# Transposing probabilities in two halves by rows, with the causal masks behind them

## The chip, the cores and the metric

The kernel runs on one core of a Trainium2 chip. Its time is device microseconds of one execution. The engines are named as the profile names them: PE (TensorE; its weight loads are PEld), DVE (VectorE), ACT (ScalarE), POOL (GpSimd) and SP (which here issues the DMAs). L612 is line 612 of the kernel.

## The reference, cut to what matters

Decayed causal attention over 8 x 8 heads of 576 tokens and 64 columns, in float32, and a feed-forward layer behind it:

```python
scores = (1.0 / np.sqrt(D)) * np.matmul(q, k.transpose(0, 1, 3, 2))
cum = np.cumsum(np.log(np.clip(f, 0.0001, 1.0)), axis=-1)
decay = cum[:, :, :, None] - cum[:, :, None, :]
scores = np.where(causal, -1000000000.0, scores + decay)   # causal: column > row
attn = np.exp(scores - np.max(scores, axis=-1, keepdims=True))
attn = attn / (np.sum(attn, axis=-1, keepdims=True) + 1e-09)
x = np.matmul(attn, v)                                     # then (4608, 512)
h = x @ w_in
y = (h * erf(softplus(h))) @ w_out
```

## The kernel before, in words

The program has two stages. The first is attention, 64 steps t = 0 to 63 and a few that drain the pipeline. The second is the feed-forward layer, of which a unit has 36 matmuls into y (L242) and up to 42 into four banks (L184). The y matmuls take as weights the gate tiles (gh and gl, L225 to L232), which lie on the right side of SBUF behind the four small tiles `line0` to `line3` (L341).

A step of attention works on one half of a pair of heads: p, half = t // 2, t % 2. The 576 query rows of a head are cut into five blocks; an even step has the blocks 4 and 1, an odd step 3, 2 and 0. Both heads of the pair, j = 0 and 1, are done side by side. For a given half the work goes through six steps:

- `scores(t)`, L528: the two heads' products with q and k on 64 rows of the array each, into two buffers s0 and s1 of two PSUM banks; there are just these two buffers, so step t + 1 writes over what step t left. Right behind them (L544) matmuls of 128 rows with a constant add the mask of the diagonal blocks: two in an even step from t = 2 on, four in an odd one.
- `reduce(t, j)`, L561: DVE adds the decay, writes the sum to `pr` and finds the row's bound; two (even) or three (odd) instructions a head.
- `exps(t, j)`, in step t + 1: the exponentials on ACT.
- `normalize(t)`, in step t + 2: a sum and a reciprocal on DVE, then four or six products on POOL.
- `transposes(t, a)`, in step t + 3: the probabilities are transposed on PE, 128 x 128 each, into bank a: 12 of them for an even t (a = 0, 1, 2), 13 for an odd one, whose short bank 3 comes first. Three PSUM buffers (tag "t") take turns. `evacuate(t, a)` copies the banks to `pt`: ACT does 0, 1 and 3 and bank 2 of an even t, DVE bank 2 of an odd one.
- `values(t)`, in step t + 4: matmuls with 64 columns of the array for each head (L630); `store` copies the result on DVE.

So even steps transpose an odd half, with bank 3, and odd steps an even half. Steps 0 to 2 also have `lead(4)`, four filler matmuls behind the masks, and step 0 has `spread` (four matmuls that ACT copies to the decays). On the side DVE, ACT and POOL convert the weights (`words`, `joined`, `out_high` and others).

Every engine's order is the order in which the code issues (a manual schedule). PE goes through scores, masks, transposes, values; DVE through normalize, store, reduce (j = 0), reduce (j = 1), bank 2, conversions; ACT through exps (j = 0), the first evacuations, exps (j = 1), the other evacuations. The array has three modes: 64 rows (scores), 128 rows (masks, transposes) and 64 columns (values).

Of the kernel before, what the change touches and what calls it, by code (L numbers as in the profile page):

```python
# [11 lines left out]
F32 = mybir.dt.float32  # L12
# [10 lines left out]
P = 128  # L23
# [8 lines left out]
END = [64, 192, 320, 448, 576]  # L32
PAD = 64

BLOCKS = [[4, 1], [3, 2, 0]]


TOFF = {4: 0, 1: 1152, 3: 0, 2: 896, 0: 1536}
TCOLS = [1536, 1664]
# [3 lines left out]
SCOL = {4: 192, 1: 0, 0: 448, 3: 0, 2: 512}  # L43


BANKS = [[[(4, 0, 0), (4, 0, 1), (4, 0, 2), (4, 0, 3)], [(4, 1, 0), (4, 1, 1), (4, 1, 2), (4, 1, 3)],
# [274 lines left out]
def attention_moe(ctx, tc, q2, k2, vp, f, w_in, w_out, out):  # L321
    nc = tc.nc
# [7 lines left out]
    ident = const.tile([P, P], F32, name="ident")  # L330
    make_identity(nc, ident)
    eye = const.tile([P, P], BF16, name="eye")
# [5 lines left out]
    upper = const.tile([P, P], BF16, name="upper")  # L338
    nc.vector.tensor_copy(out=upper, in_=low)
    edge = ctx.enter_context(tc.tile_pool(name="edge", bufs=1, side="right"))  # L340
    lines = [edge.tile([P, 32 if n else 24], F32, name=f"line{n}") for n in range(4)]  # L341
    for line in lines:
        nc.vector.memset(line, 1e-9)
    cum_d = dram.tile([B * H, S], F32, name="cum_d")
# [19 lines left out]
    def queue_transfers():  # L364
        for out, in_ in moves:
            nc.sync.dma_start(out=out, in_=in_)
        moves.clear()
# [102 lines left out]
    with ExitStack() as ph:  # L470
        early = ExitStack()
        wk = ph.enter_context(tc.tile_pool(name="wk", bufs=2))
        io = early.enter_context(tc.tile_pool(name="io", bufs=3, side="right"))
        ps_s = early.enter_context(tc.tile_pool(name="ps_s", bufs=2, space=PSUM, side="right"))
        ps_t = ph.enter_context(tc.tile_pool(name="ps_t", bufs=3, space=PSUM))
# [11 lines left out]
        pairs, stats, probs, vals, raw_scores, pts, banks, held = {}, {}, {}, {}, {}, {}, {}, {}  # L487
# [40 lines left out]
        def scores(t):  # L528


            p, half = divmod(t, 2)
            q, k = pairs[p][:2]
            s = [ps_s.tile([P, 1024], F32, name=f"s{t}_{j}", tag="s") for j in range(2)]
            for at, i, k0, k1 in PARTS[half]:
                for j in range(2):
                    h = slice(64 * j, 64 * j + 64)
                    nc.tensor.matmul(out=s[j][:, at:at + k1 - k0], lhsT=q[h, PAD + START[i]:PAD + END[i]],  # L537
                                     rhs=k[h, k0:k1], start=i > 0, stop=k1 < END[i] or i == 4 and p > 0)
            for j in range(2):
                for i in BLOCKS[half]:  # L540
                    if i == 3 or i == 4 and p:
                        continue
                    first = max(0, START[i])
                    nc.tensor.matmul(out=s[j][:, SCOL[i] + first:SCOL[i] + END[i]], lhsT=eye,  # L544
                                     rhs=upper[:, first - START[i]:], start=False, stop=True)
            raw_scores[t] = s
            probs[t] = wk.tile([P, TCOLS[half]], F32, name=f"pr{t}", tag=f"pr{half}")
            n = len(BLOCKS[half])
            stats[t] = lines[t % 4][:, :6 * n].rearrange("p (a j m) -> p a j m", a=3, j=2)

        def mask(p, i):

# [4 lines left out]
        def row(t, i, j):  # L557

            return probs[t][:, TOFF[i] + j * END[i]:TOFF[i] + (j + 1) * END[i]]

        def reduce(t, j):  # L561
            p, half = divmod(t, 2)
            c, s, st = pairs[p][2], raw_scores[t][j], stats[t]
            for m, i in enumerate(BLOCKS[half]):
                to, score, decay_ = (x.rearrange("p (k n) -> p k n", n=64) for x in (
                    row(t, i, j), s[:, SCOL[i]:SCOL[i] + END[i]], c[:, j, :END[i]]))
                nc.vector.tensor_tensor_reduce(  # L567
                    out=to[:, ::-1] if j else to, in0=score, in1=decay_, scale=-0.125, scalar=BIG,
                    op0=ALU.add, op1=ALU.min, accum_out=st[:, 0, j, m:m + 1])
            if j:  # L570
                del raw_scores[t]
                if half:
                    del pairs[p]

        def exps(t, j):
            st = stats[t]
            for m, i in enumerate(BLOCKS[t % 2]):
                seg = row(t, i, j)
                nc.scalar.activation(out=seg, in_=seg, func=AF.Exp, bias=st[:, 0, j, m:m + 1], scale=-1.0,  # L579
                                     accum_out=st[:, 1, j, m:m + 1])  # L580
# [13 lines left out]
        def transposes(t, a):  # L594

            half = t % 2
            if t not in pts:
                pts[t] = wk.tile([P, 1600 if half else 1536], F32, name=f"pt{t}", tag=f"pt{half}", bufs=1)
            banks[t, a] = b = ps_t.tile([P, 512], F32, name=f"t{t}_{a}", tag="t")
            for n, (i, j, *ch) in enumerate(BANKS[half][a]):  # L600

                at = TOFF[i] + (i * P if j is None else 2 * END[i] - ch[0] * P - P if j else ch[0] * P)
                nc.tensor.transpose(out=b[:, n * P:(n + 1) * P], in_=probs[t][:, at:at + P], identity=ident)  # L603

        def evacuate(t, a):
            b, pt = banks.pop((t, a)), pts[t]
            if a == 3:
                (nc.vector.tensor_copy if t == NH - 1 else nc.scalar.copy)(out=pt[:, 1536:], in_=b[:, 64:128])
            elif a == 2 and t % 2 or t == NH - 1:
                nc.vector.tensor_copy(out=pt[:, 512 * a:512 * a + 512], in_=b)  # L610
            else:
                nc.scalar.copy(out=pt[:, 512 * a:512 * a + 512], in_=b)  # L612
            if a == (3 if t == NH - 1 else 2):
                del probs[t]

# [46 lines left out]
        first = wk.tile([P, 2, P], F32, name="first", tag="pr1")[:B * H]  # L662
# [22 lines left out]
        for t in range(NH + 2):  # L685
            there = [0 <= t - n < NH for n in range(6)]
            p, half = divmod(t, 2)
            if half == 0 and there[2]:
                load_values(p - 1)
            if half == 0 and t + 4 < NH:  # L690
                load(p + 2)
                load_decays(p + 2)
            queue_transfers()
            if t == X0:
                moe.load_x(0)
                moe.later = moe.x_steps(0)
            if half and NH - 32 < t < NH - 16:
                moe.load_wi_part(*divmod((t - NH + 32) // 2, 4))
            if there[2]:
                normalize(t - 2)  # L700
            if half and t + 1 < NH:
                mask(p + 1, 4)
            if there[5] and t < NH + 2:
                store(t - 5)
            if t >= NH:
                units(t)
            if there[0]:
                scores(t)
            if t == 0:
                spread(pairs[0][2], cum)  # L710
            if t < 3:
                lead(4)
            if there[1]:
                exps(t - 1, 0)
            if there[0]:
                reduce(t, 0)
            if there[3]:
                order = range(3) if half else (3, 0, 1, 2)
                for a in order:
                    transposes(t - 3, a)  # L720
                for a in order[:-2]:
                    evacuate(t - 3, a)
            if there[4]:
                values(t - 4)
            if there[1]:
                exps(t - 1, 1)
            if there[0]:
                reduce(t, 1)
            if there[3]:
                for a in range(1, 3):  # L730
                    evacuate(t - 3, a)
            if there[0] and not half:
                mask(p, 3)
            todo = work.pop(t, [])
            while t > X0 and moe.later:
                step = moe.later[0]
                if (half if step[0] == moe.high else not half or columns(todo + [step]) > LIMIT):
                    break
                todo.append(moe.later.pop(0))
                if not half:  # L740
                    break
            convert(todo)
            if t > NH and there[4]:
                store(t - 4)
            if t == NH - 1:
                moe.load_x(1)
            if t == NH - 1:
                early.close()
                moe.ep = moe_pools.enter_context(tc.tile_pool(name="ep", bufs=2, side="right", reuse_waits="tile"))
                moe.ps_h = moe_pools.enter_context(tc.tile_pool(name="ps_h", bufs=1, space=PSUM, side="right", reuse_waits="tile"))  # L750
# [75 lines left out]
```

## Time and profile before

| | |
|---|---|
| median of 3 runs | 1083.06 us (1082.73 to 1083.41) |
| the profiled execution | 1082.37 us |
| its span, first to last instruction | 1080.5 us |
| granted PE clock | 1.00 |
| PE busy | 1073.0 us, 99% of the span |
| DVE, ACT, POOL busy | 829.2, 745.1 and 733.6 us |
| attention stage | to about 330 us |

A line of the timeline has the start, the length, the engine, the line of the code, the operation, out<-in, the shape and a count of equal instructions that follow each other; in brackets stand the idle time before it and what ended it. A float32 matmul of scores or values leaves two records, a transpose one. A matmul's end is modelled, and the next one can start before it. A line of a group ends in busy us, mean ns of one, and the engine's idle us before it.

### The profile page before, as it was taken

To read this page: it belongs to the slowest core of one execution; us is meant where nothing else is said; L and a number is where in the kernel's file an instruction comes from. 1 tells how busy PE (TensorE), PEld (TensorE's weight loads), DVE (VectorE), ACT (ScalarE), POOL (GpSimd) and SP (SyncE) were. 2 spreads that over 40 slices of the span, in tenths; PEclk is the share of its full clock that TensorE was granted. 3 is DMA by queue.
4 is the path that set the end of the run, shared out by engine and by line. 5 is a ranking of instruction groups with operands and counts; after the bars stand their busy time and mean duration, and the time that the engine had idled before them with its cause. 6 is when DMAs were issued, how large, how long until landed. Compare 5 with 4: busy or idle time off the path is not lost.

```text
span 1080.5 us, 21954 instructions
## 1 busy us (share of the span) xinstructions
PE 1073.0 (99%) x7480; PEld 944.3 (87%) x7480; DVE 829.2 (77%) x1878; ACT 745.1 (69%) x1624; POOL 733.6 (68%) x887
## 2 busy tenths in 40 slices
PE   8999999999999999999999999999999999999998
PEld 6888888888889899889889988988998899889887
DVE  6888888887667988987887986686766767676665
ACT  5898988998877657666665666566566655656553
POOL 3786998989856879698887878555363455536322
PEclk9999999999999999999999999999999999999999
DMA  8888999998747697878969787686858668684742
GB/s 290 280 297 278 352 315 331 349 315 299 257 144 266 234 333 265 327 291 286 341 245 340 259 299 273 229 319 221 308 182 304 261 233 303 237 317 165 250 181 98
DMA packets 87055, 293.69 MB, mean 272 GB/s; under 512 B 8992, under 2 KB 25376, under 8 KB 74912
## 3 DMA queue, kind: packets, MB, share of 16 engines
q1 hardware_dynamic: 86800, 292.00, 76.1%
q8 instruction: 60, 0.98, 0.3%
q14 instruction: 51, 0.42, 0.1%
q10 hardware_dynamic: 144, 0.29, 0.1%
HBM read 240.73 MB, written 51.53 MB: 270 GB/s over the span
## 4 chain that ended last, share of the span: by engine, by line
PE 95%; ACT 2%; DVE 2%; issue 1%; POOL 0%; POOLq 0%; ACTq 0%; DVEq 0%
PE y L242 37%; PE pha L184 9%; PE phy L184 9%; PE phx L184 9%; PE s L537 9%; PE o L630 8%; PE t L603 7%; PE phb L184 5%; PE s L544 1%; ACT pr L579 1%; DVE pr L567 1%; ACT pt L612 1%; PE lead L510 1%; ACT whi L425 0%; DVE wtop L393 0%
## 5 line engine op out<-in xcount | busy, mean ns | idle before, releaser
L231 POOL TENSOR_TENSOR gl<-e,gh 128x384 fp32r<-128x384 f32 x192 | 217.2, 1160 | 267.4 <-PE y L242 172.4
L242 PE MATMUL y<-wo,gh 128*128 128x512 f32 x1152 | 361.5, 395 | 0.1
L242 PEld LDWEIGHTS y<-wo,gh 128*128 128x128 f32 x1152 | 216.3, 189 | 47.4 <-DVE ys L263 0.8
L242 PE MATMUL y<-wo,gl 128*128 128x512 f32 x576 | 227.8, 396 | 0.0
L263 DVE TENSOR_TENSOR ys<-y,ys 128x512 f32<-128x512 f32 x252 | 171.7, 686 | 54.0 <-PE y L242 53.4
L591 POOL TENSOR_SCALAR pr<-pr,line 128x576 f32<-128x576 f32 (+4 forms) x320 | 170.7, 554 | 44.1 <-DVE line L587 23.8
L579 ACT ACTIVATE pr<-pr,line 128x576 f32<-128x576 f32 (+3 forms) x320 | 177.2, 562 | 2.2 <-DVE line L567 2.2
L567 DVE CUSTOM_DVE_ANT_0 pr<-s,c 128x576 f32<-128x576 f32 (+3 forms) x320 | 136.7, 487 | 50.7 <-issue 14.3
L230 ACT CAST gh<-e 128x384 fp32r<-128x384 f32 x192 | 94.1, 513 | 86.1 <-DVE e L223 79.2
L242 PEld LDWEIGHTS y<-wo,gl 128*128 128x128 f32 x576 | 108.5, 188 | 25.2
L213 ACT ACTIVATE e<-u 128x384 f32<-128x384 f32 x144 | 75.0, 522 | 76.6 <-DVE u L190 72.5
L184 PE MATMUL pha<-xs,wi 128*128 128x384 f32 x576 | 116.0, 336 | 0.0
L184 PE MATMUL phy<-xs,wi 128*128 128x384 f32 x576 | 115.4, 335 | 0.0
L184 PE MATMUL phx<-xs,wi 128*128 128x384 f32 x576 | 115.3, 335 | 0.0
L223 DVE TENSOR_TENSOR e<-e,u 128x384 f32<-128x384 f32 x144 | 114.3, 795 | 0.0
L537 PE MATMUL s<-k,q 64*128 64x320 f32 (+4 forms) x768 | 110.7, 407 | 1.5 <-DVE line L567 1.1
L612 ACT COPY pt<-t 128x512 f32<-128x512 f32 x158 | 88.5, 582 | 31.2 <-PE t L603 30.9
L184 PEld LDWEIGHTS pha<-xs,wi 128*128 128x128 f32 x576 | 102.0, 188 | 4.4
L630 PEld LDWEIGHTS o<-pt,v 128*64 128x64 f32 x1920 | 93.7, 137 | 11.4 <-DVE line L567 7.6
L630 PE MATMUL o<-pt,v 128*64 128x128 f32 (+1 forms) x1920 | 102.5, 259 | 0.5 <-DVE xo L639 0.5
L213 ACT ACTIVATE e<-pha 128x384 f32<-128x384 f32 x48 | 23.6, 491 | 114.3 <-PE pha L184 114.3
L184 PEld LDWEIGHTS phx<-xs,wi 128*128 128x128 f32 x576 | 101.2, 188 | 0.0
(75 smaller groups left out, 1733.0 us busy)
## 6 DMA issues: line engine op xcount, KB each, us to landing
wi<-wi_d SPq DMA_DIRECT2D x46, 1792.0 KB, 7.5
wo<-wo_d SPq DMA_DIRECT2D x48, 1024.0 KB, 5.4
v<-in_vp_dram SPq DMA_DIRECT2D x32, 576.0 KB, 4.6
r<-xt_d SPq DMA_DIRECT2D x48, 384.0 KB, 9.1
c<-cum_d SPq DMA_DIRECT2D x62, 288.0 KB, 6.7
q<-in_q_dram SPq DMA_DIRECT2D x32, 320.0 KB, 5.0
k<-in_k_dram SPq DMA_DIRECT2D x32, 288.0 KB, 6.2
part_d<-ys SPq DMA_DIRECT2D x36, 256.0 KB, 6.2
```

What stands on the lines that cost most here:

```text
L184: nc.tensor.matmul(out=ps, lhsT=wi[:, w, n, kd], rhs=xs[:, x, kd], start=not part and kd == 0 and i == 0, stop=kd == 1 and i == 2, skip_gr ...
L213: nc.scalar.activation(out=e_, in_=h[c], func=AF.Softplus)
L223: nc.vector.tensor_mul(e_, e_, h_)
L231: nc.gpsimd.tensor_tensor(out=gl, in0=e_, in1=gh.bitcast(F32), op=ALU.subtract)
L242: nc.tensor.matmul(out=y, lhsT=x[:, cs], rhs=wo[:, i, w], start=i == 0 and n == 0, stop=i == 1 and n == 2)
L263: nc.vector.tensor_tensor(out=ys, in0=y, in1=ys, op=ALU.add)
L537: nc.tensor.matmul(out=s[j][:, at:at + k1 - k0], lhsT=q[h, PAD + START[i]:PAD + END[i]], rhs=k[h, k0:k1], start=i > 0, stop=k1 < END[i] or ...
L567: nc.vector.tensor_tensor_reduce(out=to[:, ::-1] if j else to, in0=score, in1=decay_, scale=-0.125, scalar=BIG, op0=ALU.add, op1=ALU.min, ...
L579: nc.scalar.activation(out=seg, in_=seg, func=AF.Exp, bias=st[:, 0, j, m:m + 1], scale=-1.0, accum_out=st[:, 1, j, m:m + 1])
L591: nc.gpsimd.tensor_scalar(out=seg, in0=seg, scalar1=st[:, 2, j, m:m + 1], scalar2=1.0, op0=ALU.mult, op1=ALU.mult)
L612: nc.scalar.copy(out=pt[:, 512 * a:512 * a + 512], in_=b)
L630: nc.tensor.matmul(out=o[h, to:to + width], lhsT=v[:, ch, h], rhs=pt[:, at[j]:at[j] + width], start=n == 0, stop=n == len(parts) - 1, skip ...
```

## The change: what it does

Of the 12 or 13 transposes of a step the eight of banks 0 and 1 are each done as two halves: 64 rows of the probabilities with a 64 x 64 corner of the identity, so that a half gives 64 columns. The upper rows' halves go to bank 0 and the lower rows' to bank 1, in turn. They are in the 64-row mode of the scores and are issued right behind them. The masks, now a function of their own, follow the halves; then bank 3 (even steps) and bank 2 as before. In steps 0 to 2, which have no transposes, the masks follow `lead(4)`. The copies of the banks 0 and 1 put every run of 64 back in its place. `line3` is 64 instead of 32 columns wide, by which the tiles behind it on that side move by 128 bytes.

```diff
-    lines = [edge.tile([P, 32 if n else 24], F32, name=f"line{n}") for n in range(4)]
+    lines = [edge.tile([P, (24, 32, 32, 64)[n]], F32, name=f"line{n}") for n in range(4)]
...
+        def mask_scores(t):
+            p, half = divmod(t, 2)
             for j in range(2):
                 for i in BLOCKS[half]:
                     if i == 3 or i == 4 and p:
                         continue
                     first = max(0, START[i])
-                    nc.tensor.matmul(out=s[j][:, SCOL[i] + first:SCOL[i] + END[i]], lhsT=eye,
+                    nc.tensor.matmul(out=raw_scores[t][j][:, SCOL[i] + first:SCOL[i] + END[i]], lhsT=eye,
                                      rhs=upper[:, first - START[i]:], start=False, stop=True)
...
-            banks[t, a] = b = ps_t.tile([P, 512], F32, name=f"t{t}_{a}", tag="t")
-            for n, (i, j, *ch) in enumerate(BANKS[half][a]):
-
-                at = TOFF[i] + (i * P if j is None else 2 * END[i] - ch[0] * P - P if j else ch[0] * P)
-                nc.tensor.transpose(out=b[:, n * P:(n + 1) * P], in_=probs[t][:, at:at + P], identity=ident)
+            for n in (a, a + 1) if a == 0 else (a,) if a > 1 else ():
+                banks[t, n] = ps_t.tile([P, 512], F32, name=f"t{t}_{n}", tag="t")
+            pieces = [TOFF[i] + (i * P if j is None else 2 * END[i] - ch[0] * P - P if j else ch[0] * P)
+                      for n in ((0, 1) if a == 0 else (a,) if a > 1 else ()) for i, j, *ch in BANKS[half][n]]
+            for n, at in enumerate(pieces):
+                if a:
+                    nc.tensor.transpose(out=banks[t, a][:, n * P:(n + 1) * P], in_=probs[t][:, at:at + P], identity=ident)
+                else:
+                    for r in range(2):
+                        h = slice(64 * r, 64 * r + 64)
+                        nc.tensor.transpose(out=banks[t, r][:, n * 64:(n + 1) * 64], in_=probs[t][h, at:at + P],
+                                            identity=ident[h, h])
 
         def evacuate(t, a):
             b, pt = banks.pop((t, a)), pts[t]
+            to = pt[:, 512 * a:min(512 * a + 512, pt.shape[1])]
+            if a < 2:
+                to, b = pt[:, :1024].rearrange("p (n r q) -> p n r q", n=8, r=2)[:, :, a], b.rearrange("p (n q) -> p n q", n=8)
...
+            order = range(3) if half else (3, 0, 1, 2)
+            if there[3]:
+                transposes(t - 3, 0)
             if there[0]:
+                mask_scores(t)
                 reduce(t, 0)
             if there[3]:
-                order = range(3) if half else (3, 0, 1, 2)
                 for a in order:
-                    transposes(t - 3, a)
+                    if a:
+                        transposes(t - 3, a)
                 for a in order[:-2]:
                     evacuate(t - 3, a)
```

PE in the even step t = 24, from the last scores on, before. s24_0 and s24_1 are the score buffers of the two heads, t21_0 to t21_3 the banks of the half that is transposed, o20 the values; in brackets stand the engines that a row waits for.

```order
L537 MATMUL s24_1_2027<-k12_1678,q12_1677 128x192
L544 MATMUL s24_0_2026<-upper_75,eye_68 128x128
L544 MATMUL s24_1_2027<-upper_75,eye_68 128x128
L603 MATMUL t21_3_2043<-ident_63,pr21_1790 128x128 [waits Activation_49,Pool_49]
L603 MATMUL t21_0_2045<-ident_63,pr21_1790 128x128 [waits Activation_49]
L603 MATMUL t21_0_2045<-ident_63,pr21_1790 128x128 x3
L603 MATMUL t21_1_2050<-ident_63,pr21_1790 128x128 [waits Activation_49]
L603 MATMUL t21_1_2050<-ident_63,pr21_1790 128x128 x3
L603 MATMUL t21_2_2055<-ident_63,pr21_1790 128x128 [waits Activation_49]
L603 MATMUL t21_2_2055<-ident_63,pr21_1790 128x128 x3
L630 MATMUL o20_2062<-pt20_1963,v10_1839 64x128 [waits DMAHW6_49,DVE_49]
```

The same place after the change (the rows of two of the eight pairs of halves, the other six pairs and the loads of the mask's constant left out):

```order
L537 MATMUL s24_1_2195<-k12_1814,q12_1813 128x192
L612 MATMUL t21_0_2207<-ident_63,pr21_1930 128x64 [waits Activation_49,Pool_49]
L612 MATMUL t21_1_2208<-ident_63,pr21_1930 128x64 [waits Activation_49]
L612 MATMUL t21_0_2207<-ident_63,pr21_1930 128x64 [waits Pool_49]
L612 MATMUL t21_1_2208<-ident_63,pr21_1930 128x64
L551 MATMUL s24_0_2194<-upper_75,eye_68 128x128
L551 MATMUL s24_1_2195<-upper_75,eye_68 128x128
L608 MATMUL t21_3_2229<-ident_63,pr21_1930 128x128 [waits Activation_49,Pool_49]
L608 MATMUL t21_2_2231<-ident_63,pr21_1930 128x128 [waits Activation_49]
L608 MATMUL t21_2_2231<-ident_63,pr21_1930 128x128 x3
L643 MATMUL o20_2238<-pt20_2116,v10_1991 64x128 [waits DMAHW6_49,DVE_49]
```

The masks have moved behind the 16 halves, and t21_2 follows directly on t21_3; both before and after t21_2 waits for ACT, whose copy of bank 3 frees its buffer.

PE in step 1, at the program's start, before (s1_0 and s1_1 are again the score buffers, lead the filler):

```order
L537 MATMUL s1_1_261<-k0_174,q0_173 128x64
L544 MATMUL s1_0_260<-upper_75,eye_68 128x128
L544 MATMUL s1_0_260<-upper_75,eye_68 128x64
L544 MATMUL s1_1_261<-upper_75,eye_68 128x128
L544 MATMUL s1_1_261<-upper_75,eye_68 128x64
L510 MATMUL lead_273<-ident_63 128x128 [waits PE_49]
L510 MATMUL lead_273<-ident_63 128x128 x3
L537 MATMUL s2_0_307<-k1_178,q1_177 128x320 [waits DMAHW3_49,DMAHW4_49,DVE_49,PE_49]
```

And after:

```order
L537 MATMUL s1_1_261<-k0_174,q0_173 128x64
L510 MATMUL lead_269<-ident_63 128x128 x4
L551 MATMUL s1_0_260<-upper_75,eye_68 128x128
L551 MATMUL s1_0_260<-upper_75,eye_68 128x64
L551 MATMUL s1_1_261<-upper_75,eye_68 128x128
L551 MATMUL s1_1_261<-upper_75,eye_68 128x64
L537 MATMUL s2_0_307<-k1_178,q1_177 128x320 [waits DMAHW3_49,DMAHW4_49,DVE_49,PE_49]
```

Here the filler has moved ahead of the four masks.

More of the change, by code (lines that the diff above doesn't have):

```diff
@@ L538, in scores @@
                                      rhs=k[h, k0:k1], start=i > 0, stop=k1 < END[i] or i == 4 and p > 0)
+            raw_scores[t] = s
+            probs[t] = wk.tile([P, TCOLS[half]], F32, name=f"pr{t}", tag=f"pr{half}")
+            n = len(BLOCKS[half])
+            stats[t] = lines[t % 4][:, :6 * n].rearrange("p (a j m) -> p a j m", a=3, j=2)
+        def mask_scores(t):
+            p, half = divmod(t, 2)
             for j in range(2):
@@ L543, in scores @@
                     first = max(0, START[i])
-                    nc.tensor.matmul(out=s[j][:, SCOL[i] + first:SCOL[i] + END[i]], lhsT=eye,
+                    nc.tensor.matmul(out=raw_scores[t][j][:, SCOL[i] + first:SCOL[i] + END[i]], lhsT=eye,
                                      rhs=upper[:, first - START[i]:], start=False, stop=True)
[L546 to L549, printed above, removed]
         def mask(p, i):
@@ L609, in evacuate @@
             elif a == 2 and t % 2 or t == NH - 1:
-                nc.vector.tensor_copy(out=pt[:, 512 * a:512 * a + 512], in_=b)
+                nc.vector.tensor_copy(out=to, in_=b)
             else:
-                nc.scalar.copy(out=pt[:, 512 * a:512 * a + 512], in_=b)
+                nc.scalar.copy(out=to, in_=b)
             if a == (3 if t == NH - 1 else 2):
```

## The prediction

> **What bounds the kernel now.** First the page's chain of work that ended last, by engine. Then the sums of a window, the attention stage.
>
> ```profile
> PE 95%; ACT 2%; DVE 2%; issue 1%; POOL 0%; POOLq 0%; ACTq 0%; DVEq 0%
> 24.00:330.00 306.00, 304.84 (x3617) 258.55 (x3616) 240.87 (x935) 272.47 (x830) 250.93 (x435) 1.00 0.86 294
> ```
>
> The columns of the second, behind the stretch and its 306 us, are the busy us of PE, PEld, DVE, ACT, POOL. TensorE is busy for 304.84 of them, so a saving on it looks like a saving of time. But in this stage, the only one with transposes, the other engines are 79 to 89% busy too (240.87 to 272.47), and what matters is how soon each comes round again. So I read the timeline of one pair of steps, t = 24 (even) from 120.64 and t = 25 (odd) from 125.25 to 130.12; most of the 29 pairs from t = 4 on take these 9.48 us.
>
> ```profile
> 120.64 1.57 PE L537 MATMUL s<-k,q 64*128 64x320 f32 x12
> 122.14 0.28 PE L544 MATMUL s<-upper,eye 128*128 128x128 bf16 x2
> 122.26 1.59 PE L603 MATMUL t<-ident,pr 128*128 128x128 f32 x13
> 122.50 0.76 DVE L567 CUSTOM_DVE_ANT_0 pr<-s,c 128x576 f32<-128x576 f32 x1 [1.19 <-POOL wa L421]
> 122.58 0.21 ACT L608 COPY pt<-t 128x64 f32<-128x64 f32 x1
> 123.78 1.54 PE L630 MATMUL o<-pt,v 128*64 128x128 f32 x28
> 124.42 0.08 DVE L567 DVE_READ_ACCUMULATOR2_ANT line<- 128x1 f32 x1
> 125.25 1.73 PE L537 MATMUL s<-k,q 64*128 64x448 f32 x12
> 126.91 0.34 PE L544 MATMUL s<-upper,eye 128*128 128x128 bf16 x4
> 127.09 1.51 PE L603 MATMUL t<-ident,pr 128*128 128x128 f32 x12
> 127.32 0.62 DVE L567 CUSTOM_DVE_ANT_0 pr<-s,c 128x448 f32<-128x448 f32 x1
> 128.53 1.66 PE L630 MATMUL o<-pt,v 128*64 128x128 f32 x32
> 129.53 0.08 DVE L567 DVE_READ_ACCUMULATOR2_ANT line<- 128x1 f32 x1
> 130.12 0.54 PE L537 MATMUL s<-k,q 64*128 64x320 f32 x2
> ```
>
> A second loop is hidden here. VectorE starts its reductions 0.36 us after the first mask of an even step (122.14 to 122.50) and 0.41 after that of an odd one (126.91 to 127.32). The view names POOL at 122.50, but the distance of 0.36 comes back in every even step, so the masks release it. The reductions take 2.00 (to 124.42 + 0.08) and 2.29 us (to 129.53 + 0.08). The next scores overwrite the banks that they read. In the pair above TensorE comes back 0.75 and 0.51 us after they ended, so the loop isn't felt; at the program's start it is:
>
> ```profile
> 9.38 0.76 DVE L567 CUSTOM_DVE_ANT_0 pr<-s,c 128x576 f32<-128x576 f32 x1 [2.90 <-ACT c L520]
> 9.79 1.16 PE L510 MATMUL lead<-ident 128*128 128x128 f32 x8
> 13.28 0.34 PE L544 MATMUL s<-upper,eye 128*128 128x128 bf16 x4
> 13.46 1.14 PE L510 MATMUL lead<-ident 128*128 128x128 f32 x8
> 13.70 0.62 DVE L567 CUSTOM_DVE_ANT_0 pr<-s,c 128x448 f32<-128x448 f32 x1 [0.78 <-PE s L544]
> 15.90 0.08 DVE L567 DVE_READ_ACCUMULATOR2_ANT line<- 128x1 f32 x1
> 16.13 1.53 PE L537 MATMUL s<-k,q 64*128 64x320 f32 x10 [0.37 <-DVE line L567]
> ```
>
> At 13.70 VectorE is named as waiting for the masks, and 0.15 us after its reductions (15.98 to 16.13) TensorE goes on.
>
> **The change, part by part.** *The halves.* The rates come from the groups by form and from two short stretches of the timeline that hold one form alone.
>
> ```profile
> L603 PE MATMUL t<-ident,pr 128*128 128x128 f32 x800 | 100.6, 275 | 0.4
> L630 PE MATMUL o<-pt,v 128*64 128x64 f32 x640 | 29.4, 222 | 0.0
> 122.59 0.93 PE L603 MATMUL t<-ident,pr 128*128 128x128 f32 x7
> 110.29 0.52 PE L630 MATMUL o<-pt,v 128*64 128x64 f32 x12
> ```
>
> Seven transposes end 0.93 after the first began; less one's 0.275, six spacings make 0.655, or 0.109 each. Eight take 0.87 us. A half moves 64 columns and runs beside its partner on other rows of the array. No row shows such a transpose; the nearest is the pair of 64-column value matmuls, side by side by columns: 12 in 0.52, less 0.222, five spacings in 0.30, or 0.058 a pair (the partner 0.007 behind). Eight pairs: 0.47 us. Bounds: 0.03 a pair if the load no longer counts (half of the above), 0.109 if a half costs what a whole did. I take 0.058. TensorE alone saves 0.87 - 0.47 = 0.40 us a step.
>
> *The masks.* They were right behind the scores and now come behind the halves. The switch of array mode is there either way (scores end, as modelled, at 122.21 and 126.98, masks start 0.07 before that; a stream of one mode goes on 0.16 before), so the number of switches stays and the masks come later by the eight pairs: 0.47 us. VectorE's reductions wait in its queue with the copies out of PSUM and the weight conversions behind them, and the next scores wait for them.
>
> *The odd tile's last banks.* In an even step TensorE issued t_3, then t_0 and t_1, then t_2 into t_3's buffer. Eight transposes covered ScalarE's copy of t_3 out. Now t_2 comes directly behind t_3, and waits. Priced: t_3 starts at 122.26, its copy at 122.58 (0.32) and takes 0.21; from its end to t_2 the nearest row is an even step in which that copy came late:
>
> ```profile
> 103.56 0.20 ACT L608 COPY pt<-t 128x64 f32<-128x64 f32 x1
> 103.81 0.42 PEld L603 LDWEIGHTS t<-ident,pr 128*128 128x128 f32 x4
> ```
>
> 0.05. So t_2 starts 0.58 after t_3 where TensorE needs 0.11: a stall of 0.47 that eats the even step's 0.40. Values and the next scores are queued behind it.
>
> *Sum of an ordinary pair,* from the even scores. Even: masks at 1.50 + 0.47 = 1.97, t_3 at 2.09, t_2 at 2.67, its four and the switch 0.53 (four spacings of 0.109 and 0.09), values 1.47 (123.78 to 125.25): next scores at 4.67 (before 4.61). By the other loop: 1.97 + 0.36 + 2.00 + 0.15 = 4.48, so the copy decides. Odd: masks at 1.66 + 0.47 = 2.13, + 0.41 + 2.29 + 0.15 = 4.98, against TensorE's 4.87 - 0.40 = 4.47: the reductions decide. Together 9.65, about 0.03 less since only one of the two score buffers comes late: 9.62, or 0.14 longer than 9.48.
>
> *Pairs in which VectorE is late already.* In nine odd steps conversions keep it from starting with the masks; the first and the last:
>
> ```profile
> 40.38 0.34 PE L544 MATMUL s<-upper,eye 128*128 128x128 bf16 x4
> 41.59 0.62 DVE L567 CUSTOM_DVE_ANT_0 pr<-s,c 128x448 f32<-128x448 f32 x1
> 252.61 0.34 PE L544 MATMUL s<-upper,eye 128*128 128x128 bf16 x4
> 253.49 0.62 DVE L567 CUSTOM_DVE_ANT_0 pr<-s,c 128x448 f32<-128x448 f32 x1
> ```
>
> There the whole queue moves by the even masks' 0.47: about 0.40 each, some being less late. Four more pairs take 9.79 now, since ScalarE is late with t_3; a t_3 that comes later hides that, so 0. The remaining 16 pay 0.14. Stage: 9 x 0.40 + 16 x 0.14 = 5.8.
>
> *The start.* For t = 0 to 2 the fillers (lead) now stand ahead of the masks, and this stretch goes by the loop. t = 0: the spread and the lead move up by the masks' place, some 0.4 (their 0.34 at 13.28 and a switch), the masks come behind the lead, at 9.79 - 0.4 + 1.16 - 0.16 = 10.4, reductions at 10.8 for 9.38: 1.4. For t = 1 and 2 a lead's 1.14 - 0.16 = 0.98 each; t = 3 has its halves, 0.47. Together 3.8 us.
>
> *The end, the evacuations, the gate tiles.* The last steps have no reductions behind them: 0.4 x 4 saved, less the new t_3 wait and a switch of mode each: -0.4 (0 to -1.6). A copy now writes runs of 64 with gaps; the nearest rows cost the same with gaps (L639) as without (L642): 0. The gate tiles feed the y matmuls as weights; 48 blocks, of which most read 8.37 in the chain and these are the ends:
>
> ```profile
> L642 DVE COPY xo<-o 128x256 f32<-128x256 f32 x32 | 13.4, 418 | 7.2 <-PE o L630 7.2
> L639 DVE COPY xo<-o 128x256 f32<-128x256 f32 x32 | 13.1, 411 | 0.4 <-PE o L630 0.4
> 589.90 8.52 PE y L242 x36
> 605.71 8.36 PE y L242 x36
> ```
>
> So between -0.5 and +7.2 us; no row ties any of it to an address, and I take 0.
>
> Sum: 5.8 + 3.8 - 0.4 = +9.2. The profiled execution took 1082.37 (span 1080.5 and 1.9 around it), 0.7 under the median of 1083.06: 1091.6 on its scale, **1092** on the median's. About 2 us (0.2%) is what can be told from no change.
>
> **Rivals.** *The time goes down with TensorE* (faster). If the first reduction, over columns that no mask touches, waited for the scores alone, the later masks would hide behind its 0.76 us (at 122.50). The even step would keep its copy (4.67), the odd one would go by TensorE (4.47): 9.14 a pair, -0.34 in 20 pairs, nothing at the start: 1076; without the t_3 wait too, 1067. For it speak the 95% of the chain; against it the constant 0.36 and 0.41, and the row at 13.70. It decides if reductions start before the masks end. Chance 0.12.
>
> *Two halves cost as much as a whole* (slower by more). The weights of a half still have 128 columns.
>
> ```profile
> L603 PEld LDWEIGHTS t<-ident,pr 128*128 128x128 f32 x800 | 86.3, 140 | 2.0 <-ACT pt L608 1.3
> L537 PEld LDWEIGHTS s<-k,q 64*128 64x128 f32 x768 | 73.4, 186 | 29.8 <-issue 14.8 <-PE lead L510 0.5
> L630 PEld LDWEIGHTS o<-pt,v 128*64 128x64 f32 x1920 | 93.7, 137 | 11.4 <-DVE line L567 7.6 <-issue 2.9 <-DVE xo L639 1.0
> ```
>
> If a pair then takes the whole's 0.109, the masks come 0.87 later: 0.80 more a pair of steps, 29 x 0.80 = 23: 1115. Against it: a transpose's load reads 140 ns, like one of 64 columns (137), not like the scores' 128 (186). The Trainium skill (TensorE: Matmul & The Clock Gate, LDWEIGHTS) speaks for this rival and against the change: a load's time goes by its columns, about P / 1.2 ns, whatever the rows; an estimate from it is 107 ns a half. By that rule, the trace's 140 beside 186 disagrees, but no run here shows a half. Chance 0.10.
>
> *Both effects cancel.* If a pair of halves takes 0.03, the masks are 0.24 late, pairs come down to 9.2 and the late pairs and the start cost 5: between 1078 and 1086, about the old time. Chance 0.16, of which 0.06 faster, 0.06 same, 0.04 slower.
>
> **How the numbers follow.** The forecast has 0.62. Its own range is 1086 to 1099: the pair from 9.55 to 9.75, the gate tiles' upper end in part, the start by 1 us. The range 1075 to 1100 adds the cancelling case and the upper end of the first rival; beyond it lie the second rival and part of the first, under 0.2. Of the forecast 0.04 falls below its own range, within 0.2% of no change. Faster 0.12 + 0.06 = 0.18; same 0.06 + 0.04 = 0.10; slower 0.58 + 0.04 + 0.10 = 0.72.
>
> **What the changed profile would show.** Right: eight pairs of halves in about 0.63 us as modelled; masks 1.95 to 2.0 after even scores; VectorE still 0.36 and 0.41 behind the masks; t_2's load 0.05 behind ScalarE's copy of t_3; odd steps near 4.95 with the scores released by VectorE; the seventh scores some 4 us later than now; TensorE less busy from 24 to 330. Wrong: reductions that start ahead of the masks, pairs of steps under 9.4, halves 0.109 apart, or a change of the y blocks after 340.

## The result and the profile after

| | before | after |
|---|---|---|
| median | 1082.89 us (1082.52 to 1083.41) | 1091.74 us (1090.05 to 1094.47) |
| the profiled execution | 1082.37 us | 1091.56 us |
| its span | 1080.5 us | 1089.7 us |
| mean granted PE clock | 1.00 | 0.995 |

The ratio is 1.0084 (95% interval 1.0066 to 1.0102): slower by 0.84%, where 1092 us was forecast. The chain by engine, of the changed kernel, has hardly moved:

```profile
PE 93%; DVE 2%; ACT 2%; issue 1%; DMA 1%; POOL 0%; SPq 0%; ACTq 0%; DVEq 0%; POOLq 0%
```

The sums of its window 24 to 330 us (busy us of PE, PEld, DVE, ACT, POOL, then the granted clock) tell more:

```profile
24.00:330.00 306.00, 292.53 (x3979) 242.12 (x3980) 232.73 (x940) 265.93 (x819) 244.08 (x431) 0.99 0.86 288
```

TensorE has 12 us less to do in the same 306 us and yet is later. The timeline of a pair of steps, t = 24 (even) from 131.12 and t = 25 (odd) from 136.35 to 140.85, with the lines between left out:

```profile
131.12 1.72 PE L537 MATMUL s<-k,q 64*128 64x320 f32 x10
131.40 0.08 DVE L570 DVE_READ_ACCUMULATOR2_ANT line<- 128x1 f32 x1
131.60 0.83 PEld L537 LDWEIGHTS s<-k,q 64*128 64x128 f32 x8 [0.19 <-issue]
132.85 0.81 PE L612 MATMUL t<-ident,pr 64*128 64x64 f32 x13
133.59 0.28 PE L551 MATMUL s<-upper,eye 128*128 128x128 bf16 x2
133.71 0.28 PE L608 MATMUL t<-ident,pr 128*128 128x128 f32 x1
133.95 0.76 DVE L570 CUSTOM_DVE_ANT_0 pr<-s,c 128x576 f32<-128x576 f32 x1 [1.74 <-POOL wa L421]
134.03 0.21 ACT L621 COPY pt<-t 128x64 f32<-128x64 f32 x1 [0.81 <-PE t L608]
134.29 0.42 PEld L608 LDWEIGHTS t<-ident,pr 128*128 128x128 f32 x4 [0.49 <-ACT pt L621]
134.88 1.54 PE L643 MATMUL o<-pt,v 128*64 128x128 f32 x28
136.35 1.73 PE L537 MATMUL s<-k,q 64*128 64x448 f32 x12
137.91 0.67 PE L612 MATMUL t<-ident,pr 64*128 64x64 f32 x16
138.52 0.34 PE L551 MATMUL s<-upper,eye 128*128 128x128 bf16 x4
138.92 0.62 DVE L570 CUSTOM_DVE_ANT_0 pr<-s,c 128x448 f32<-128x448 f32 x1 [0.34 <-PE s L551]
140.85 1.50 PE L537 MATMUL s<-k,q 64*128 64x320 f32 x8
141.13 0.09 DVE L570 DVE_READ_ACCUMULATOR2_ANT line<- 128x1 f32 x1
```

The reductions still start 0.36 (133.59 to 133.95) and 0.40 (138.52 to 138.92) behind the masks, and t_2 loads 0.05 behind the end of ScalarE's copy of t_3 (134.24 to 134.29). The scores of an even step now start in two parts: the first head's at 131.12, the second's only behind the reductions of the odd step, which end at 131.48 (its loads at 131.60, its matmul, in the single record, at 131.63). Seen from the first scores the steps take 5.23 and 4.50; of the steps from 7 on, each taken with the one before it, 40 of 57 give 9.72 or 9.73, where before 27 of 57 gave 9.48.

The program's start in the timeline; the first row is the fillers before, the others are of the changed kernel:

```profile
1.36 4.38 PE L510 MATMUL lead<-ident 128*128 128x128 f32 x22 [1.36 <-POOL ident masks.py:199]
1.36 5.07 PE L510 MATMUL lead<-ident 128*128 128x128 f32 x22 [1.36 <-POOL ident masks.py:199]
7.12 1.57 PE L537 MATMUL s<-k,q 64*128 64x320 f32 x12 [0.69 <-DMA k<-in_k_dram]
11.69 0.39 PE L551 MATMUL s<-upper,eye 128*128 128x128 bf16 x4
12.12 0.76 DVE L570 CUSTOM_DVE_ANT_0 pr<-s,c 128x576 f32<-128x576 f32 x1 [5.51 <-PE s L551]
13.31 2.65 PE L537 MATMUL s<-k,q 64*128 64x448 f32 x12 [1.24 <-DVE line L570]
18.57 0.77 PE L537 MATMUL s<-k,q 64*128 64x320 f32 x2 [1.35 <-issue]
24.99 3.32 PE L537 MATMUL s<-k,q 64*128 64x448 f32 x9 [1.22 <-DVE line L570]
37.59 1.73 PE L537 MATMUL s<-k,q 64*128 64x448 f32 x12
```

And three windows of it, with the granted clock third from the right:

```profile
19.70:25.00 5.30, 4.07 (x21) 3.25 (x21) 2.61 (x9) 2.32 (x8) 2.27 (x4) 0.60 1.01 293
25.00:32.90 7.90, 7.06 (x40) 5.24 (x40) 4.86 (x22) 3.85 (x12) 4.84 (x9) 0.62 0.66 247
20.80:31.00 10.20, 8.98 (x49) 7.14 (x47) 4.51 (x19) 3.17 (x9) 6.00 (x13) 0.50 0.80 252
```

TensorE has holes of 1.2 to 1.4 us a step, and its clock falls: the 0.60 and 0.62 are means of stretches with 1.00 and with 0.50, and the 0.50 lasts from 20.8 to 31.0. Before, these steps had 1.00. Step 5's scores begin at 37.59 for 29.14. The first scores, at 7.12 for 5.67, come late too: the 22 fillers ahead of them take 5.07 for 4.38 (in the single records the last six of them come 0.21 us apart, where before they come 0.11 apart), and 0.69 is a wait for the load of k.

The feed-forward stage was to stay as it is. Two blocks of y matmuls in the chain, before:

```profile
825.26 8.37 PE y L242 x36
840.92 8.37 PE y L242 x36
```

and after:

```profile
821.45 8.20 PE y L242 x36
836.96 8.20 PE y L242 x36
```

A unit takes 15.51 instead of 15.66 (836.96 - 821.45; 840.92 - 825.26). This I had not expected. The two profiled executions, cut at the same events:

| stretch | forecast | measured |
|---|---|---|
| to the first scores (5.67, after 7.12) | 0 | +1.5 |
| from there to step 5's scores (23.47, after 30.47) | +3.8 | +7.0 |
| steps 5 to 63 (279.07, after 285.68) | +5.8 | +6.6 |
| step 63 to the first y (30.90, after 30.81) | -0.4 | -0.1 |
| first to last y block (720.79, after 715.32) | 0 | -5.5 |
| rest | 0 | -0.3 |
| sum | +9.2 | +9.2 |

The rows of y are those of the chain; the last one holds two blocks. The sum came out; the first scores, the start and the y blocks did not.

### The profile page after: what moved, and what is told of

Read it like the earlier page. It is cut to its first block, busy times and chain, and to the rows that moved or that the text cites. A ratio compares the mean times of both kernels' runs of the same rounds, so it can differ in the third digit from the quotient of the medians.

```text
span 1089.7 us, 22980 instructions
## 1 busy us (share of the span) xinstructions
PE 1066.3 (98%) x7992; PEld 938.1 (86%) x7992; DVE 809.0 (74%) x1878; ACT 744.2 (68%) x1624; POOL 727.4 (67%) x887
## 4 chain that ended last, share of the span: by engine, by line
PE 93%; DVE 2%; ACT 2%; issue 1%; DMA 1%; POOL 0%; SPq 0%; ACTq 0%; DVEq 0%; POOLq 0%
PE y L242 35%; PE s L537 10%; PE pha L184 9%; PE phx L184 9%; PE phy L184 9%; PE o L643 8%; PE phb L184 4%; PE t L608 3%; PE t L612 3%; PE s L551 1%; ACT pt L621 1%; DVE pr L570 1%; ACT pr L582 0%; DMA k<-in_k_dram 0%; DMA c<-cum_d 0%
## 5 line engine op out<-in xcount | busy, mean ns | idle before, releaser
L242 PE MATMUL y<-wo,gh 128*128 128x512 f32 x1152 | 356.3, 390 | 0.2 <-DVE ys L263 0.2
L242 PE MATMUL y<-wo,gl 128*128 128x512 f32 x576 | 225.1, 391 | 0.0
L594 POOL TENSOR_SCALAR pr<-pr,line 128x576 f32<-128x576 f32 (+4 forms) x320 | 166.8, 542 | 60.1 <-DVE line L590 39.0
L537 PE MATMUL s<-k,q 64*128 64x320 f32 (+4 forms) x768 | 124.8, 411 | 5.7 <-DVE line L570 3.2
L537 PEld LDWEIGHTS s<-k,q 64*128 64x128 f32 x768 | 83.1, 188 | 37.9 <-issue 26.1
```

What stands on the lines that cost most here:

```text
L242: nc.tensor.matmul(out=y, lhsT=x[:, cs], rhs=wo[:, i, w], start=i == 0 and n == 0, stop=i == 1 and n == 2)
L594: nc.gpsimd.tensor_scalar(out=seg, in0=seg, scalar1=st[:, 2, j, m:m + 1], scalar2=1.0, op0=ALU.mult, op1=ALU.mult)
```

## The experiments

Three questions: what shortens the y blocks, what the start costs beyond the masks, and whether the pairs are held by the two loops of the forecast. All times are medians; the kernel before had 1083.63, 1083.82 and 1083.34 us beside the three groups of runs.

### The y blocks: gate_only, gate_48, narrow, wo_shift, both_shift

gate_only takes the kernel before and one line of the change; gate_48 has 48 columns there; narrow is the changed kernel with 32.

```diff
-    lines = [edge.tile([P, 32 if n else 24], F32, name=f"line{n}") for n in range(4)]
+    lines = [edge.tile([P, (24, 32, 32, 64)[n]], F32, name=f"line{n}") for n in range(4)]
```

> The kernel before with line3 64 instead of 32 columns wide, nothing else. In the changed kernel a unit of the feed-forward stage takes 15.51 us where it took 15.65. If the place of the gate tiles makes that, the units take 15.51 here too and the time falls by about 46 x 0.14 = 6.4, to 1076.5 us. As the prediction priced the move (0, at most 7.2 more), the units stay at 15.65 and the time at 1083, and the shorter units come from something that the new attention stage leaves behind.

> The kernel before with line3 48 columns wide, so that the tiles behind it move by 64 bytes instead of 128. If what counts is the distance, in parts: about half of the gain, 1080. If it is one of two or more places that are good or bad as a whole: 15.65 and 1083, or 15.51 and 1076.5. If the place is nothing: 1083.

> The changed kernel with line3 back at 32 columns. If the place of the gate tiles makes the shorter units, they take 15.65 again and the time rises by 6.4, to about 1098 us; the attention stage stays as it is (scores of step 63 at 323 us). If the place is nothing: 1091.7.

gate_only: 1077.20 us, ratio 0.9942 (0.9928 to 0.9957), units of 15.51:

```profile
822.92 8.20 PE y L242 x36
838.43 8.20 PE y L242 x36
```

gate_48: 1084.91 us, 1.0012 (1.0002 to 1.0021), blocks of 8.40 and units of 15.70, slightly worse than before. narrow: 1099.17 us, 1.0143 (1.0126 to 1.0159), units of 15.65 again. So the place of the gate tiles is worth 6.4 us without the new attention stage. With it the medians differ by 7.4, of which in the profiles 6.3 lie between the first and the last y matmul (738.17 and 731.89); in the rest is the start, where narrow's step 5 comes at 39.67 for 37.59, although its attention stage was expected to stay as it is. And a move by half the distance gains nothing. wo_shift leaves the gate tiles and moves wo, the other operand of the same matmuls; both_shift moves both.

```diff
+    ctx.enter_context(tc.tile_pool(name="pad", bufs=1)).tile([P, 32], F32, name="pad")
     moe.wop = ctx.enter_context(tc.tile_pool(name="wop", bufs=1, reuse_waits="tile"))
```

> The kernel before with 128 bytes of padding on the left side, ahead of wo, the moving operand of the y matmuls; the gate tiles stay where they were. Before, the gate tiles start at multiples of 512 bytes of a partition and wo at 128 past one; in the kernel gate_only (fast) both lie 128 past a multiple of 256. Theory: what counts is how the weights and the moving operand lie to each other; then the padding, which puts both at multiples of 256, gives the same gain, 15.51 a unit and 1077. Rival: the place of the gate tiles alone counts: 15.65 and 1083.

> The kernel wo_shift with line3 64 columns wide as well: gate tiles 128 past a multiple of 256 bytes, wo at a multiple of 256. If their distance counts, they are apart again: 15.65 a unit and 1083. If the place of the gate tiles alone counts: 15.51 and 1077.

wo_shift: 1077.05 us, 0.9947 (0.9930 to 0.9964), units of 15.50:

```profile
821.14 8.19 PE y L242 x36
```

both_shift: 1084.25 us, 1.0011 (1.0001 to 1.0020):

```profile
826.85 8.40 PE y L242 x36
```

Moving either operand by 128 bytes gains 6 us, moving both gains nothing. Each padding moves other tiles too (q, k, c, u and e with the gate tiles, ys with wo), but the y matmuls read only these two operands. So by these runs what counts is how weights and moving operand lie to each other (the places are those of the built programs, no trace shows them): with both at the same place within 256 bytes a block takes 8.19 or 8.20 us, 128 bytes apart 8.37 (before) or 8.40 (both_shift), 64 bytes apart 8.40. In the single records, by position in the block, the fast kernels start most matmuls 0.226 or 0.227 us apart, gate_48 0.233 or 0.234, both_shift 0.229 and 0.237 in turn, and the kernel before 0.228 to 0.233 with one of 0.240 or 0.241 every seventh. The Trainium skill (TensorE: Matmul & The Clock Gate, Step-by-step: what each phase is for) says that TensorE has two independent read ports, so that loading weights takes nothing from the running matmul; by that rule the addresses should not matter, and these five runs show that they do. By what mechanism no run here shows.

### The start: start_masks, start_fill

start_masks puts the masks of the first three steps back ahead of the filler; start_fill leaves them late and adds a second filler behind them.

```diff
 # start_masks
             if there[0]:
                 scores(t)
+                if t < 3:
+                    mask_scores(t)
...
             if there[0]:
-                mask_scores(t)
+                if t > 2:
+                    mask_scores(t)
                 reduce(t, 0)
 # start_fill
             if there[0]:
                 mask_scores(t)
+                if t < 4:
+                    lead(4)
                 reduce(t, 0)
```

> The changed kernel with the masks of the steps 0 to 2 back behind their scores, ahead of the filler. In the changed kernel the scores of step 5 begin 8.45 us later than before, of which the prediction had 3.8 from the later masks. Theory: the other 4.6 are the lower granted clock (0.60 from 19.7 to 32.9 us), which comes from the holes that TensorE has while VectorE reduces. Then both go here: granted clock 1.00 from the start on, scores of step 5 at about 30 us (0.5 to 1 later than before, for the halves of step 3), time 1084. Rival: the clock falls for another reason (the narrow halves, or chance); then only the 3.4 of the masks go: scores of step 5 at 34, time 1088, a clock of about 0.6 still there.

> The changed kernel with a second lead(4) behind the masks of the steps 0 to 3, where TensorE stands idle for 1.2 to 1.6 us until VectorE has reduced; the masks stay late. The fillers take 1.0 us each and fit the holes. If the holes lower the granted clock: clock 1.00 instead of 0.60 up to 33 us, and about 4 us less than the changed kernel, 1087 to 1088. If the clock falls for another reason, or plays no part: still 0.60, and 1091.7 or a little more.

start_masks: 1084.89 us, 1.0017 (1.0007 to 1.0026), 6.9 less than the changed kernel. The clock in the window of its steps 2 and 3:

```profile
19.10:24.60 5.50, 4.29 (x40) 2.94 (x40) 4.39 (x20) 3.03 (x10) 4.29 (x9) 1.00 1.03 407
```

Its step 5:

```profile
30.39 1.73 PE L537 MATMUL s<-k,q 64*128 64x448 f32 x12
```

From its first scores (6.26) to step 5 it takes 24.13, 0.7 more than before; the steps 3 and 4 have their masks late. start_fill: 1089.29 us, 1.0057 (1.0041 to 1.0074), where 1087 to 1088 was expected, with these windows:

```profile
19.70:25.00 5.30, 5.14 (x44) 3.91 (x43) 3.63 (x14) 1.77 (x5) 2.73 (x6) 1.00 1.03 403
25.00:32.90 7.90, 7.24 (x90) 5.94 (x86) 7.08 (x25) 6.60 (x22) 6.89 (x12) 1.00 0.81 279
```

The scores of its step 5:

```profile
32.90 1.73 PE L537 MATMUL s<-k,q 64*128 64x448 f32 x12
```

The fillers alone bring the clock back to 1.00. From its first scores (5.66) to step 5 it takes 27.24: 3.2 less than the changed kernel's 30.47, and 3.8 more than the 23.47 of before. So 3.8 of the start are the late masks, 3.2 are the clock. The median fell by 2.5 and not by 4; in this trace 2.7 us are lost again between the steps 5 and 63, most of it near 286 us, where TensorE waits 1.4 for nothing that the profile shows. The changed kernel and narrow, the two with holes, had mean clocks of 0.992 to 0.998 in each of their executions, all other kernels 0.997 to 1.000. The size of the holes is not the whole rule: in whole_late's profile (below) the clock is 0.50 from 28.0 to 34.7 behind holes of at most 0.88 since its first scores, while start_masks and bank2_first, with holes of that size too, keep 1.00.

### The pairs: masks_first, bank2_first, whole_late, halves_last

All four have the wide `line3`, so the 6 us of the y blocks stand in their times.

masks_first puts every step's masks right behind its scores and leaves the halves behind them.

```diff
             if there[0]:
                 scores(t)
+                mask_scores(t)
...
-                mask_scores(t)
                 reduce(t, 0)
```

> The changed kernel with the masks of all steps back right behind the scores; the halves follow them, at the price of two more changes of array mode (about 0.1 a step by the nearest gaps). Theory: what makes the odd step of 5.01 (from its scores to the second head's scores of the next step) is the loop of masks, reductions and scores. Then it falls to TensorE's 4.57, the even step goes from 4.72 to 4.82 (its wait for ScalarE's copy of t_3 stays), a pair takes 9.39 instead of 9.73, and with the start back as before (7 us) the time is 1076 us. Rival: the place of the masks plays no part in the pairs; then the switches make it 9.93 a pair and 1090 us.

1084.80 us, 1.0010 (1.0001 to 1.0019), the time of start_masks; the usual pair takes 9.81. An even step's t_2 and an odd step:

```profile
127.50 0.66 PE L608 MATMUL t<-ident,pr 128*128 128x128 f32 x4 [0.30 <-ACT pt L621]
129.56 1.73 PE L537 MATMUL s<-k,q 64*128 64x448 f32 x12
131.22 0.34 PE L551 MATMUL s<-upper,eye 128*128 128x128 bf16 x4
131.49 0.72 PE L612 MATMUL t<-ident,pr 64*128 64x64 f32 x16
132.14 0.66 PE L608 MATMUL t<-ident,pr 128*128 128x128 f32 x4
```

Neither expectation held. From the masks to the halves it takes 0.27 (131.22 to 131.49), and the halves with the switch behind them 0.65 (to 132.14); in the changed kernel the halves took 0.61 up to the masks (137.91 to 138.52) and there was no further switch. The odd step takes 4.76 for 4.50. The two added changes of mode cost 0.13 each, not 0.05. The loop is gone (the scores of both heads run in one group of 12 again), but the switches cost as much, and t_2 at 127.50 still waits for the copy. By its time this run settles nothing.

bank2_first is start_masks with the order of the last banks turned round in even steps:

```diff
-            order = range(3) if half else (3, 0, 1, 2)
+            order = range(3) if half else (0, 2, 3, 1)
...
-                for a in order[:-2]:
+                for a in ((0, 3) if not half else order[:-2]):
```

> The kernel start_masks with t_2 ahead of t_3 in even steps, and ScalarE copying bank 0 ahead of bank 3: t_2 gets the free buffer, and t_3 waits for the copy of bank 0. Theory: the even step is set by the wait of t_2 for ScalarE's copy of t_3 (0.58 from t_3 to t_2). Then TensorE does the four t_2 in that time and waits some 0.3 for one t_3 instead: a pair takes 9.48 instead of 9.73, the time 1084.9 - 7 = 1078. Rival: that wait is covered, since the reductions hold the scores in any case: 9.73 and 1085.

1080.62 us, 0.9976 (0.9965 to 0.9986); the usual pair takes 9.53:

```profile
155.83 0.28 PE L551 MATMUL s<-upper,eye 128*128 128x128 bf16 x2
155.95 1.04 PE L608 MATMUL t<-ident,pr 128*128 128x128 f32 x5
156.92 1.54 PE L643 MATMUL o<-pt,v 128*64 128x128 f32 x28
```

From masks to values 1.09 us instead of 1.29 (133.59 to 134.88 above): the 0.20 arrive in the pair. The even step is set by the wait for ScalarE's copy.

whole_late is start_masks with the eight transposes whole again, in the place of the halves:

```diff
-                    for r in range(2):
-                        h = slice(64 * r, 64 * r + 64)
-                        nc.tensor.transpose(out=banks[t, r][:, n * 64:(n + 1) * 64], in_=probs[t][h, at:at + P],
-                                            identity=ident[h, h])
+                    nc.tensor.transpose(out=banks[t, n // 4][:, n % 4 * P:(n % 4 + 1) * P], in_=probs[t][:, at:at + P],
+                                        identity=ident)
```

> The kernel start_masks with the eight transposes of banks 0 and 1 whole again (128 x 128, 0.109 each as before the change), in the same place ahead of the masks. Theory: the pair is the sum of two loops, both of which contain what stands ahead of the masks; 0.87 us of whole transposes for the 0.50 that eight pairs of halves take adds 0.37 to each: odd step 5.38, even step 5.09, a pair 10.47 instead of 9.73, and the time 1084.9 + 28 x 0.74 = 1106 us. Rival: the reductions' loop alone decides one step of the two, and the other has slack: 10.1 a pair, 1095.

The copies of the banks 0 and 1 are again those of before. 1107.66 us, 1.0236 (1.0221 to 1.0251); 45 of the 57 pairs take 10.56 (the profiled execution is 3 us over the median, with the fall of the clock told above):

```profile
151.67 1.73 PE L537 MATMUL s<-k,q 64*128 64x448 f32 x12
154.25 0.33 PE L551 MATMUL s<-upper,eye 128*128 128x128 bf16 x4
154.65 0.62 DVE L570 CUSTOM_DVE_ANT_0 pr<-s,c 128x448 f32<-128x448 f32 x1 [0.81 <-PE s L551]
```

The masks come 2.58 behind the scores instead of 2.17, the reductions again 0.40 behind them, and a pair is 0.83 longer: twice the 0.41. Both loops hold what stands ahead of the masks. It also shows that the halves, in this place, are worth 22.8 us against whole transposes (1107.66 - 1084.89).

halves_last puts the masks right behind the scores and the halves at the step's end, ahead of the next scores, whose array mode they share; ScalarE copies the banks 0 and 1 at its end of the step.

```diff
             if there[0]:
                 scores(t)
+                mask_scores(t)
...
             if there[4]:
                 values(t - 4)
+            if there[3]:
+                transposes(t - 3, 0)
...
-                for a in range(1, 3):
+                for a in range(2 if half else 3):
                     evacuate(t - 3, a)
```

> The changed kernel with the masks back right behind the scores, t_3 and t_2 behind them, then the values, and the halves last, right ahead of the next scores, whose mode they share; ScalarE copies the banks 0 and 1 at its end of the step. As many changes of mode as before, no wait of t_2 for t_3 (another buffer is free), masks as early as before. If the halves' 0.40 a step is real and only their place ate it: even step 4.61 - 0.40 = 4.21, odd step 4.51 by the loop of reductions, a pair 8.7 to 8.9, and the time 1084.9 - 29 x 0.9 = 1059 (1053 to 1064). Rival: ScalarE (89% busy in this stage) or VectorE's queue becomes the bound: a pair of 9.1 to 9.3, 1067 to 1073.

1065.59 us, 0.9831 (0.9817 to 0.9846): faster than both kernels. Of the 18.2 us against the kernel before, 5.8 lie in the y blocks (731.93 from the first to the last matmul, before 737.69) and 12.3 between the steps 5 and 63 (266.81, before 279.07). A pair of steps late in the stage:

```profile
279.11 1.68 PE L537 MATMUL s<-k,q 64*128 64x448 f32 x12
287.84 1.51 PE L537 MATMUL s<-k,q 64*128 64x448 f32 x8
```

The sums of a window, and three rows of step 49, whose pair takes 10.34, with the lines between left out:

```profile
24.00:300.00 276.00, 267.70 (x3907) 224.72 (x3904) 229.09 (x915) 260.23 (x804) 249.90 (x427) 1.00 0.92 315
234.25 0.34 PE L551 MATMUL s<-upper,eye 128*128 128x128 bf16 x4
235.32 0.43 DVE L386 TENSOR_SCALAR wtop<-wtop 128x512 int32<-128x512 int32 x1
236.30 0.61 DVE L570 CUSTOM_DVE_ANT_0 pr<-s,c 128x448 f32<-128x448 f32 x1
```

The last pairs (steps 57 to 63) take 8.73 (279.11 to 287.84), as the theory had it; the mean from step 5 to 63 is 9.20. In between stand pairs of up to 10.3, and the time lies between the two expectations. Over the window ScalarE is 94% and POOL 91% busy (260.23 and 249.90 of 276), VectorE 83%, and yet the longer pairs go by VectorE. In step 49 it reduces 2.05 behind the masks (234.25 to 236.30): weight conversions (L384 to L402) and what stands behind them in its queue keep it until then, with no pause over 0.04. Of the 29 pairs that start at an odd step, 24 have such a late start, by 0.06 to 1.64 over the usual 0.41, and less this excess every pair but one takes 8.70 to 8.75. So each expectation holds a part: the halves' saving is there, and VectorE's queue takes some of it back.

## Why the forecast came out, point by point

- **A pair of halves** was put at 0.058 us and takes 0.063 (16 in 0.67, less 0.22 for one and 0.01 for the partner, over seven spacings). An odd step of TensorE alone went from 4.87 to 4.50, 0.37 of the 0.40. The rival that a half costs a whole one is out. The rule of the Trainium skill behind it (TensorE: Matmul & The Clock Gate, LDWEIGHTS: a load takes about P / 1.2 ns, P its columns; for 128 an estimate of 107 ns) would not let a pair go below 0.107; the trace disagrees.
- **Masks hold the reductions**: right, 0.36 and 0.40 in both kernels, and the rival with reductions that start on the scores alone is out.
- **The even step's copy** was right: 0.58 from t_3 (133.71) to t_2 (134.29), and bank2_first shows that it decides.
- **The pair**: 9.62 forecast, 9.73 measured. Measured on the second head, the odd step is 5.01 (136.35 to 141.36, 0.14 behind the last reduction) for 4.98, and the even one 4.72 (131.63 to 136.35) for 4.67. The 0.03 taken off "since only one of the two score buffers comes late" failed: the late one carries the chain, as the even masks wait for both heads. And the steps look other than forecast, since the first head's scores go ahead: 5.23 and 4.50 for 4.67 and 4.95.
- **Ordinary and late pairs**: "most of the 29 pairs" was too much, 9.48 stands in 13 (in 14, taken from odd steps, as the stretch from step 5 to 63 is). These 14 pay 0.25 each, 3.6 us, where 16 were to pay 0.14, 2.2. The nine with a late odd step pay 0.11 to 0.59, 2.8 in all, where 0.40 each, 3.6, was forecast; VectorE comes late in five odd steps only of the changed kernel. The other six pay 0.3. The 6.6 for 5.8 is thus a term too small and one too large.
- **The start**: the 3.8 of the masks are what start_fill shows. That the holes would cost clock, 3.2 more, is missing in the sum. The seventh scores are 8.1 late (42.09 for 34.01), not "some 4 us". Of the 1.5 to the first scores one half is the wait for the load of k and one half the slower fillers; first scores lay between 5.66 and 7.12 in the profiles of these kernels, with no order in it.
- **The gate tiles**: put at 0, between -0.5 and +7.2; measured -6.4 alone. This step failed, its sign too, and a change of the y blocks after 340 us stood among the signs of being wrong. "No row ties any of it to an address" was true of the rows that I looked at; the uneven spacing of the y matmuls (0.228 to 0.241, with a long one every seventh) stood in the trace of before and was not asked about.

The attention stage thus costs about what its mechanism said: +10.4 with the clock held (3.8 and 6.6) for the forecast's 3.8 and 5.8. The clock in the start and the late first scores (+4.7) and the y blocks (-5.5) nearly cancel, and to that extent the number was right by luck.

## What to carry to other kernels

A cheaper instruction pays only where nothing that others wait for is pushed behind it: ahead of the masks the halves make the usual pair of steps 0.25 us longer (9.73 for 9.48); behind the values, with the masks first again, a pair is 0.75 shorter where VectorE is in time (8.73), and 0.42 in the mean (9.20 for 9.62). When a step is moved, follow every wait that it passes, also in the first steps of the program, where a filler has a job. And an address that a change moves is a change of its own: time it alone.

## What the runs showed of the hardware

- Holes of 1.2 to 1.4 us a step (TensorE busy 73% from 13.3 to 19.7: 4.68 of 6.40) stood ahead of a granted clock of 0.50 for 10.2 us (20.8 to 31.0); with fillers in the holes it stayed at 1.00. The Trainium skill (TensorE: Matmul & The Clock Gate, Part 1: The HAM clock gate (the "warmup" mystery)) has the clock halved after an idle window of about 3.4 us. The trace has the clock halved too, but no hole of that length before it (1.36 at most, at the program's start).
- By these five runs the relative place of a matmul's weights and moving operand within 256 bytes is worth 2% of a block of 36 matmuls of 512 columns (8.19 or 8.20 against 8.37 to 8.40).
- Two more changes of array mode in a step, around the halves, make an odd step 0.26 us longer (4.76 for 4.50), 0.13 each.
- Two heads side by side on the array fell out of step when one waited for its buffer, and the halves behind them ran apart too: 13 halves took 0.81 us at 132.85, 16 in step took 0.67.
- In halves_last the busiest engines beside TensorE (ScalarE 94%, POOL 91%) did not set the longer pairs; VectorE did, at 83%, by the place of its conversions ahead of the reductions.
